# SwiGLU feed-forward: gate 0 moves to SyncE's queue, and ScalarE loads its table before its one load

## The chip, the core and the metric

The kernel runs on one core of a Trainium2 chip. A core has TensorE (matrix multiply, with a separate row for its weight loads), VectorE, ScalarE, GpSimd and SyncE. ScalarE and SyncE can both issue DMAs, each on a queue of its own; SyncE does nothing else here. The metric is the device time of one execution in microseconds, given as the median over several runs.

## The reference

The inputs are x (2048 tokens of 512 values), w_gate and w_up (512 x 1376) and w_down (1376 x 512), all in bf16:

```python
g = silu(x @ w_gate)
u = x @ w_up
return (g * u) @ w_down
```

## The kernel before

The kernel works with transposed activations: for each tile of 128 features it computes x @ w transposed, features on the partitions and tokens along the free dimension. Weights are the stationary operand and the transposed x, `xT_sb`, is the moving one. The 512 values of the contraction make four steps (`dk`) of 128, so one tile of 128 features by 512 tokens takes four matmuls into one PSUM bank. The features make ten full tiles and a rest of 96; gate and up of one tile use two banks of the eight. ScalarE applies silu to the gate bank, VectorE multiplies with the up bank and writes `hT_sb`. There are four chunks of 512 tokens; after them the rest of 96 features is handled in groups X and Y. The second stage multiplies with w_down in pieces of 32 partitions and stores 16 output tiles of 128 tokens.

What concerns the change is the start. Tokens 256 and up come transposed by a DMA (`load_x`, line 95). Tokens 0-127 and 128-255 come in their natural layout (`load_xn`, line 115, into `xn_sb`) and are transposed by TensorE with an identity matrix (line 367); VectorE and ScalarE copy the four tiles of each block to `xT_sb` in turn. The weights of the first stage come in slabs, `[(0, 1), (1, 2), (2, 4), (4, 7), (7, 11)]` in tiles of 128 features, each with one gate and one up load (line 100). Gate 0 and up 0 below are the first slab: 128 KB each.

The order is written out by hand. Before the change ScalarE's queue issues gate 0 and tokens 128-255, then a small dummy activation (line 277), whose only purpose is that ScalarE loads its function table (the ACT_TABLE_LOAD in the profile) before silu is needed. Then its list of operations starts, each waiting for TensorE. SyncE's queue issues tokens 0-127, up 0, then slabs 1 and 2-3, the transposing loads of tokens 256-383 and 384-511, the other slabs, the other tokens, w_down, and last the output stores.

TensorE begins with seven matmuls on constants (`warm`, line 358) that compute nothing that is used. Then, each step waiting only for what it reads:

- transposes of tokens 0-127, and two more constant matmuls
- gate 0 on tokens 0-127 (needs gate 0, line 326)
- transposes of tokens 128-255
- up 0 on tokens 0-127 (needs up 0)
- gate 0 and up 0 on tokens 128-255
- six tiles of slabs 1 and 2-3 on tokens 0-255, in the order gate 1, up 1, gate 2, gate 3, up 2, up 3
- gate 0 and up 0 on tokens 256-383, then on 384-511, then the other six tiles on tokens 256-511
- all other tiles on 512 tokens at once.

A load is awaited once, by the first matmul that needs it (`need`). A bank is used again when its readers are done (`free`). GpSimd makes the indices from which VectorE builds the identity, and has no load on its queue.

Of the kernel before, what the change touches and what calls it, by code (L numbers as in the profile page):

```python
# [14 lines left out]
def bass_standalone__swiglu_ffn__prompt_kernel(nc, x, w_gate, w_up, w_down, out):  # L15
# [35 lines left out]
    with ExitStack() as es:  # L51
# [33 lines left out]
        def load_sem(name):  # L85
            loads[name] = sem(f"s_{name}")
            return loads[name]
# [6 lines left out]
        def load_x(eng, name, t0, t1):  # L94
            eng.dma_start_transpose(
                xT_sb[:, :, t0:t1], xf[t0:t1, :]
            ).then_inc(load_sem(name), 16)

        def load_w(eng, name, src, base, f0, f1):
            eng.dma_start(  # L100
                w_sb[:, :, base + f0:base + f1],
                src[:, f0:f1].rearrange("(k p) f -> p k f", p=P),
            ).then_inc(load_sem(name), 16)

        slabs = [(0, 1), (1, 2), (2, 4), (4, 7), (7, NFT)]
        slab_of = {ft: a for a, b in slabs for ft in range(a, b)}

        def load_gate(eng, a, b):
            load_w(eng, f"wg{a}", w_gate, 0, a * P, min(b * P, F))

        def load_up(eng, a, b):
            load_w(eng, f"wu{a}", w_up, UPH, a * P, min(b * P, F - 32))

        def load_xn(eng, i):
            eng.dma_start(xn_sb[:, i, :], xf[i * P:(i + 1) * P, :]).then_inc(load_sem(f"xn{i}"), 16)
# [1 line left out]
        def out_rows(t):  # L117
            return of[t * P:(t + 1) * P, :]

        def loads_on_scalar(act):  # L120
            load_gate(act, *slabs[0])
            load_xn(act, 1)

        def loads_on_sync(sp):
            load_xn(sp, 0)
            load_up(sp, *slabs[0])
            for a, b in slabs[1:3]:
                load_gate(sp, a, b)
                load_up(sp, a, b)
            load_x(sp, "x0b", HT, HT + P)  # L130
            load_x(sp, "x0c", HT + P, SC)
            for a, b in slabs[3:]:
                load_gate(sp, a, b)
                load_up(sp, a, b)
            load_w(sp, "wut", w_up, F - (F - 32), F - 32, F)
            for c in range(1, NSC):
                load_x(sp, f"x{c}", c * SC, (c + 1) * SC)
            sp.dma_start(
                wd_sb[:, 0:NFF, :], w_down[0:NFF * P, :].rearrange("(k p) d -> p k d", p=P)
            ).then_inc(load_sem("wd"), 16)  # L140
            load_sem("wdt")
            for y0 in (0, 64):
                sp.dma_start(wd_sb[y0:y0 + 64, T01, :], w_down[NFF * P:F - SR, :]).then_inc(loads["wdt"], 16)
            for x0 in range(0, P, SR):
                sp.dma_start(wd_sb[x0:x0 + SR, T2, :], w_down[F - SR:F, :]).then_inc(loads["wdt"], 16)
            sp.dma_start(wd_sb[0:F_LAST, TAIL, :], w_down[NFF * P:F, :]).then_inc(load_sem("wdl"), 16)
# [104 lines left out]
        def ready(op):  # L251
            return op["ready"] if "ready" in op else (s_P, op["g"]["at"] + 1)

        def store_tiles(eng, own):
            for o, t, c0, c1, ob, copied, n in stores:
                if o == own:
                    eng.wait_ge(s_A if copied == "A" else s_D, n)
                    eng.dma_start(out_rows(t)[:, c0:c1], o_sb[ob][:, c0:c1]).then_inc(s_out[ob], 16)

        def on_sync(sp):  # L260
            loads_on_sync(sp)
            store_tiles(sp, "S")
            for i in range(NOS):
                sp.wait_ge(s_out[i], 16 * n_store[i])
# [8 lines left out]
            pool.tensor_copy(hl_sb[64:96, :], hx_sb[64:96, c, SC - P:SC]).then_inc(s_L, 1)  # L273

        def on_scalar(act):
            loads_on_scalar(act)
            act.activation(adummy[:, 0:4], zero_c, ACT.Silu)  # L277
            for op in act_ops:
                act.wait_ge(*ready(op))
                if op["kind"] == "silu":  # L280
                    if op["free"]:
                        act.wait_ge(s_D, op["free"])
                    fn = ACT.Silu
                else:
                    if op["stored"][1]:
                        act.wait_ge(*op["stored"])
                    fn = ACT.Copy
                act.activation(op["out"], op["src"], fn).then_inc(s_A, 1)  # L288
            store_tiles(act, "A")
# [199 lines left out]
        on_sync(nc.sync)  # L489
        on_gpsimd(nc.gpsimd)  # L490
        on_scalar(nc.scalar)
        on_tensor(nc.tensor)
        on_vector(nc.vector)
# [28 lines left out]
```

## Time and profile before

| what | value |
|---|---|
| time, median of 3 runs | 120.14 us (120.06 to 120.38) |
| the profiled execution's own time | 120.41 us |
| its span, first to last instruction | 119.1 us |
| TensorE busy | 116.5 us (98%) |
| VectorE busy | 38.3 us (32%) |
| ScalarE busy | 35.2 us (30%) |
| TensorE's first matmul starts | 0.77 us |
| table load on ScalarE | starts 1.79 us, takes 1.28 us |
| DMA read and written | 4.75 MB and 2.10 MB |

The profile is of one execution. Engines are PE (TensorE's matmuls), PEld (its weight loads), DVE (VectorE), ACT (ScalarE), POOL (GpSimd) and SP (SyncE). A name with q behind it (ACTq, SPq) is the engine's instruction queue, which issues DMAs and handles waits. The length of a DMA line is the time that the queue took to issue it; the data land later, and the page gives the time from the start of the issue to the landing. L326 is line 326 of the kernel. Matmuls overlap each other, so the length of one is longer than its distance to the next; the distance, or the number of matmuls in a window, tells the rate. A remark in square brackets is the time that the engine sat idle just before, and what ended it.

### The profile page before, as it was taken

How to read it: one execution, taken by the hardware profiler on the slowest of the kernel's cores; microseconds unless marked ns; L12 is line 12 of the kernel's file. 1: busy time of each engine (PE TensorE's matmuls, PEld its weight loads, DVE VectorE, ACT ScalarE, POOL GpSimd, SP SyncE). 2: the span in 40 equal slices, each digit the busy share in tenths (PEclk: the TensorE clock that was granted, in tenths of full speed). 3: DMA queues.
4: the chain of work that ended last, by engine and by line, in shares of the span. 5: the costliest groups of instructions: out<-in, count | busy, mean ns of one | idle time of the engine just before them, and what ended most of it. 6: DMA issues, size and time to landing. Idle time of an engine off the chain costs nothing.

```text
span 119.1 us, 2344 instructions
## 1 busy us (share of the span) xinstructions
PE 116.5 (98%) x1019; PEld 60.6 (51%) x1019; DVE 38.3 (32%) x61; ACT 35.2 (30%) x62; POOL 1.0 (1%) x7
## 2 busy tenths in 40 slices
PE   7999999999999999999999999999999999999993
PEld 2899544444444444444444444444444445885452
DVE  0204633444334444334453344361000044003321
ACT  3406444262343272442353432430000033003021
POOL 1000000000000000000000000001000000000000
DMA  4999989991000000000000000000000017200612
GB/s 84 296 176 347 265 178 239 265 340 29 0 6 0 0 0 0 0 6 0 0 0 6 0 0 0 0 0 6 0 6 0 0 51 235 77 0 6 204 61 88
DMA packets 17642, 8.83 MB, mean 74 GB/s; under 512 B 10624, under 2 KB 17632, under 8 KB 17632
## 3 DMA queue, kind: packets, MB, share of 16 engines
q1 hardware_dynamic: 16816, 8.33, 27.5%
q10 hardware_dynamic: 816, 0.36, 1.1%
q8 instruction: 8, 0.13, 0.4%
q14 instruction: 2, 0.02, 0.1%
HBM read 4.75 MB, written 2.10 MB: 58 GB/s over the span
## 4 chain that ended last, share of the span: by engine, by line
PE 98%; DVE 0%; issue 0%
PE bank L326 62%; PE bank L444 25%; PE bank L483 7%; PE bank L358 2%; PE bank L406 2%; PE bank L367 1%; DVE o_sb L302 0%
## 5 line engine op out<-in xcount | busy, mean ns | idle before, releaser
L326 PE MATMUL bank<-xT_sb,w_sb 128*128 128x512 bf16 (+2 forms) x384 | 73.7, 356 | 0.0
L326 PEld LDWEIGHTS bank<-xT_sb,w_sb 128*128 128x128 bf16 x384 | 37.0, 100 | 36.3
L298 DVE TENSOR_TENSOR hT_sb<-sg_sb,bank 128x512 bf16<-128x512 f32 x40 | 27.5, 687 | 40.5 <-PE bank L326 39.6
L288 ACT ACTIVATE sg_sb<-bank 128x512 f32<-128x512 f32 x40 | 23.8, 596 | 40.9 <-PE bank L326 40.8
L444 PE MATMUL bank<-wd_sb,hT_sb 32*128 32x512 bf16 x496 | 29.0, 374 | 0.0
L444 PEld LDWEIGHTS bank<-wd_sb,hT_sb 32*128 32x128 bf16 x496 | 15.2, 93 | 11.6 <-issue 0.4
L302 DVE CAST o_sb<-bank 128x512 bf16<-128x512 f32 (+1 forms) x10 | 5.7, 595 | 31.1 <-PE bank L444 25.9
L288 ACT ACTIVATE o_sb<-bank 128x512 bf16<-128x512 f32 (+1 forms) x8 | 4.3, 582 | 33.6 <-PE bank L444 27.9
L483 PE MATMUL bank<-wd_sb,hT_sb 128*128 128x512 bf16 (+2 forms) x56 | 8.1, 304 | 0.0
L483 PEld LDWEIGHTS bank<-wd_sb,hT_sb 128*128 128x128 bf16 x56 | 4.2, 97 | 4.2 <-issue 0.4
L444 PE MATMUL bank<-wd_sb,hy_sb 32*128 32x512 bf16 (+1 forms) x32 | 5.0, 371 | 0.0
L298 DVE TENSOR_TENSOR hx_sb<-sgx_sb,bank 32x512 bf16<-32x512 f32 x4 | 2.8, 692 | 3.5 <-ACT sgx_sb L288 3.5
L288 ACT ACTIVATE sgx_sb<-bank 32x512 f32<-32x512 f32 x4 | 2.3, 587 | 4.5 <-PE bank L326 4.5
L358 PE MATMUL bank<-const-bfloat16-1.0 128*128 128x512 bf16 (+1 forms) x9 | 2.9, 486 | 0.8 <-PEq L507 0.8
L444 PE MATMUL bank<-wd_sb,hx_sb 32*128 32x512 bf16 (+1 forms) x16 | 3.0, 371 | 0.0
L288 ACT ACTIVATE sgy_sb<-bank 64x512 f32<-64x512 f32 x4 | 2.4, 590 | 0.1
L358 PEld LDWEIGHTS bank<-const-bfloat16-1.0 128*128 128x128 bf16 x9 | 1.1, 140 | 2.1 <-issue 2.1
L406 PE MATMUL bank<-xT_sb,w_sb 128*64 128x512 bf16 x16 | 1.9, 382 | 0.0
L444 PEld LDWEIGHTS bank<-wd_sb,hy_sb 32*128 32x128 bf16 x32 | 1.6, 93 | 0.6
L302 DVE COPY xT_sb<-bank 128x128 bf16<-128x128 bf16 x4 | 0.9, 224 | 3.0 <-PE bank L367 3.0
L277 ACT ACT_TABLE_LOAD x1 | 1.3, 1283 | 1.8 <-issue 1.8
L406 PEld LDWEIGHTS bank<-xT_sb,w_sb 128*64 128x64 bf16 x16 | 0.8, 109 | 1.0 <-DVE hT_sb L298 0.4
(16 smaller groups left out, 7.3 us busy)
## 6 DMA issues: line engine op xcount, KB each, us to landing
out_dram<-o_sb SPq DMA_DIRECT2D x15, 128.0 KB, 1.8
wd_sb<-in_w_down_dram SPq DMA_DIRECT2D x1, 1280.0 KB, 8.3
w_sb<-in_w_gate_dram SPq DMA_DIRECT2D x1, 480.0 KB, 5.5
w_sb<-in_w_up_dram SPq DMA_DIRECT2D x1, 448.0 KB, 7.5
w_sb<-in_w_gate_dram SPq DMA_DIRECT2D x1, 384.0 KB, 4.0
w_sb<-in_w_up_dram SPq DMA_DIRECT2D x1, 384.0 KB, 4.4
w_sb<-in_w_up_dram SPq DMA_DIRECT2D x2, 128.0 KB, 3.3
w_sb<-in_w_gate_dram SPq DMA_DIRECT2D x1, 256.0 KB, 3.7
```

The costliest lines, as they stand in the source:

```text
L277: act.activation(adummy[:, 0:4], zero_c, ACT.Silu)
L288: act.activation(op["out"], op["src"], fn).then_inc(s_A, 1)
L298: ins = dve.tensor_tensor(op["out"], op["a"], op["b"], ALU.mult)
L302: ins = dve.tensor_copy(op["out"], op["src"])
L326: return pe.matmul(bank[:, n0:n1], lhsT=w_sb[:, dk, col:col + P], rhs=xT_sb[:, dk, c * SC + n0:c * SC + n1], start=(dk == 0), stop=(dk == ...
L358: pe.matmul(banks[NB - 1][:, 0:width], lhsT=ones_w, rhs=ones_m[:, 0:width], start=True, stop=True)
L367: pe.matmul(tview(i, dk), lhsT=xn_sb[:, i, dk * P:(dk + 1) * P], rhs=ident[:, :], start=True, stop=True, is_transpose=True,).then_inc(s_X, 1)
L406: ins = pe.matmul(g["bank"][y0:y1, :], lhsT=w_sb[:, dk, YC0:YC0 + 64], rhs=xT_sb[:, dk, c * SC:(c + 1) * SC], start=(dk == 0), stop=(dk == ...
L444: ins = pe.matmul(g["bank"][:, 0:c1 - c0], lhsT=h, rhs=wd_sb[r0:r0 + SR, w, c0:c1], start=(start and fk == fks[0]), stop=(stop and fk == f ...
L483: ins = pe.matmul(g["bank"][:, 0:c1 - c0], lhsT=h, rhs=w, start=(last and fk == 0), stop=(fk == (NFF if last else NFF - 1)), skip_group_ch ...
```

## The change

ScalarE no longer issues gate 0. It starts with the dummy activation, and with it the table load, and then issues the load of tokens 128-255. SyncE issues tokens 0-127, gate 0, up 0 and then everything that it issued before in the same order. No computation and no wait of another engine is changed.

```diff
-        def loads_on_scalar(act):
-            load_gate(act, *slabs[0])
-            load_xn(act, 1)
-
         def loads_on_sync(sp):
             load_xn(sp, 0)
-            load_up(sp, *slabs[0])
-            for a, b in slabs[1:3]:
+            for a, b in slabs[0:3]:
                 load_gate(sp, a, b)
                 load_up(sp, a, b)
             load_x(sp, "x0b", HT, HT + P)
...
         def on_scalar(act):
-            loads_on_scalar(act)
             act.activation(adummy[:, 0:4], zero_c, ACT.Silu)
+            load_xn(act, 1)
             for op in act_ops:
                 act.wait_ge(*ready(op))
```

## The prediction

> **What bounds the kernel now.** I read the chain of waits first, then the first ten microseconds of the timeline with the DMA issues, and last TensorE's groups in two short windows. All times are from the profiled execution, which took 120.41 us: its span of 119.1 us and 1.3 us around it. That is 0.27 us above the median of the runs shown, 120.14 us, so I sum differences and set them on the median. About 0.3% (0.36 us) is what a measurement of this kernel can tell from no change.
>
> The busy line and the chain of waits, in order of time (start, length, what):
>
> ```profile
> PE 116.5 (98%) x1019; PEld 60.6 (51%) x1019; DVE 38.3 (32%) x61; ACT 35.2 (30%) x62; POOL 1.0 (1%) x7
> ...
> 0.77 2.51 PE bank L358 x7
> 3.28 0.01 issue
> 3.29 0.58 PE bank L367 x4
> 3.88 0.21 PE bank L358 x2
> 4.09 0.46 PE bank L326 x4
> 4.55 0.47 PE bank L367 x4
> 5.01 72.96 PE bank L326 x380
> ```
>
> The chain is TensorE from end to end. From 5 us on it never leaves TensorE, so a load matters only if it makes TensorE wait, and everything that the change moves is needed in the first ten microseconds. Here is what is issued and done there (start, length, engine, line):
>
> ```profile
> 0.74 0.46 ACTq L100 DMA_DIRECT2D w_sb<-in_w_gate_dram  x1
> 0.74 0.40 SPq L115 DMA_DIRECT2D xn_sb<-in_x_dram  x1
> 1.19 0.42 SPq L100 DMA_DIRECT2D w_sb<-in_w_up_dram  x1
> 1.23 0.53 ACTq L115 DMA_DIRECT2D xn_sb<-in_x_dram  x1
> 1.79 1.28 ACT L277 ACT_TABLE_LOAD   x1 [1.79 <-issue]
> 3.08 0.20 ACT L277 ACTIVATE act_dummy<-const-float32-0.0 128x4 f32<-128x4 f32 x1
> 3.26 0.35 PEld L367 LDWEIGHTS bank<-ident,xn_sb 128*128 128x128 bf16 x4 [0.25 <-issue]
> 3.70 0.49 ACT L288 ACTIVATE xT_sb<-bank 128x128 bf16<-128x128 bf16 x2 [0.41 <-PE bank L367]
> 3.93 0.41 PEld L326 LDWEIGHTS bank<-xT_sb,w_sb 128*128 128x128 bf16 x4
> 4.40 0.34 PEld L367 LDWEIGHTS bank<-ident,xn_sb 128*128 128x128 bf16 x4
> 4.70 0.15 PEld L326 LDWEIGHTS bank<-xT_sb,w_sb 128*128 128x128 bf16 x1
> ```
>
> And the issues of 0.5 to 2.9 us with their size and the time from issue to landing:
>
> ```profile
> w_sb<-in_w_gate_dram ACTq DMA_DIRECT2D x1, 128.0 KB, 2.9
> xn_sb<-in_x_dram SPq DMA_DIRECT2D x1, 128.0 KB, 2.4
> xn_sb<-in_x_dram ACTq DMA_DIRECT2D x1, 128.0 KB, 3.1
> ```
>
> Together they give the landings. Tokens 0-127 land at 0.74 + 2.4 = 3.14 and their transposes (line 367) load weights at 3.26, so TensorE waited for them. Gate 0 lands at 0.74 + 2.9 = 3.64, 0.29 us ahead of its first weight load at 3.93, which waits for a transposed tile instead. Tokens 128-255 land at 1.23 + 3.1 = 4.33, and their transposes load weights at 4.40: just in time. Up 0 lands at 1.19 + 3.3 = 4.49 (3.3 is the median of both up loads of 128 KB) and is needed at 4.70.
>
> TensorE's rate in this stretch is read from two windows, 4.8 to 5.9 us and 6.1 to 8.6 us:
>
> ```profile
> L326 PE MATMUL bank<-xT_sb,w_sb 128*128 128x128 bf16 x11 | 1.4, 312 | 0.0
> L326 PE MATMUL bank<-xT_sb,w_sb 128*128 128x256 bf16 x24 | 2.8, 273 | 0.0
> ```
>
> Eleven matmuls of 128 columns took 1.1 us, and 24 of 256 columns 2.6 us (0.109 each): from about 6.0 us on TensorE does twice the columns in the same time. Before that it is at half rate.
>
> **The change, part by part.**
>
> 1. Tokens 0-127 stay SP's first issue at 0.74. Their companion on the other queue becomes tokens 128-255 (128 KB in rows of 1 KB) instead of gate 0 (128 KB in rows of 256 bytes). Earlier by at most TensorE's idle 0.25 us before 3.26; later by at most the 0.44 us that 128 KB take at the 296 GB/s of the window 2.6 to 6.0 us. The same bytes compete as before, so I take 0.
>
> 2. Gate 0 moves from ScalarE's first issue at 0.74 to SP's second at 1.19. With its own 2.9 us it lands at 4.09; with the 3.3 us of up 0, which had this place, queue and shape, at 4.49. The reaction at 4.40 followed a landing by 0.07, so its weight load moves from 3.93 to 4.16 or 4.56: +0.2 to +0.6. Up 0 is the nearest row, but it shared its time with gate 0, which now isn't beside it; I take the middle, +0.4.
>
> 3. Tokens 128-255 are ScalarE's only load, behind the table load and the dummy activation. The trace has no DMA issue behind a table load. If the queue merely hands both to the engine, the issue starts at about 0.80 and lands at 3.2 to 3.9 (2.4 or 3.1 us), before gate 0: cost 0. If it stands behind both (1.28 + 0.20 us), it starts at 0.74 + 1.48 = 2.22 and lands at 4.6 to 5.3, and the transposes of 4.40 go to 4.7 to 5.4: +0.3 to +1.0, not added to part 2 but taking its place where larger. Two rows speak for handing over. The dummy activation starts at 3.08, 0.01 us after the table load's end (1.79 + 1.28 = 3.07), so it was already waiting in the engine. And near the end ScalarE's queue handles a semaphore at 109.3 (line 286) that stands between two output copies, the first running from 109.24 and the second starting at 109.7. I take 0 and keep +1.0 for the range.
>
> 4. The table load itself comes forward by about 1 us and gains nothing: it and the dummy end at 3.28, and ScalarE's first real work at 3.70 waits 0.41 us for the transposes. That slack covers it and grows; without it the first tile copies would be late by what the 1.48 us overran.
>
> 5. Up 0 moves to 1.66 and lands at 1.66 + 3.3 = 4.96. Its weight load, at 4.70 plus 0.4 from part 2, is at 5.10. Covered; with the smaller delay of part 2 it would set +0.33 itself.
>
> 6. All later SP issues slip by one issue, 1.66 - 1.19 = 0.47 us (up to 0.55 further on), and each is checked against TensorE's first use after the shift of 0.2 found below. Gate 2-3 (2.75, 3.7 us): 6.45 becomes 7.00 against 6.06 + 8 x 0.109 + 0.2 = 7.13. Up 2-3 (3.30, 3.9): 7.20 becomes 7.75 against 8.00. Tokens 256-383 (3.85, 4.1): 7.95 becomes 8.50 against 8.88. Tokens 384-511 (5.24, 3.1): 8.34 becomes 8.89 against 9.33. The next gate slab (6.54, 4.0): 10.54 becomes 11.1 against 12.4. The tightest margin is 0.13 us, so 0; with no shift at all gate 2-3 would stall TensorE by 0.13 or so. The queue's longest wait is for output copies after the loads, so the slip goes no further.
>
> The sum to the first use of up 0 is +0.4 us of waiting. What it costs at the end depends on the rate. If the step to full rate stays at about 6.0 us, the work pushed past it runs in half the time, and half of the wait comes back: +0.2. If the step moves with the work, +0.4. I take +0.2, since the change leaves TensorE's start at 0.77 and its seven fill matmuls alone. In the profiled execution that would be 120.6, on the median 120.14 + 0.2 = 120.35 us: inside what can't be told from no change, near its upper edge.
>
> [...]
>
> **The rivals.**
>
> *ScalarE's queue stands behind the table load* (slower). Place: the issue of line 115. For it: no row shows a queue passing a table load. Against it: the two rows of part 3. Price: TensorE's second transposes at 4.7 to 5.4. At the late end up 0's first matmul goes from 4.81 to 5.81; of the 12 half-rate matmuls up to 6.06 two run before 6.0 and ten at 0.056 (0.109 for 256 columns, halved), ending near 6.6: +0.5. Over both ends and with the rate's step moving along, +0.15 to +1.0, most likely 120.5 to 120.7. It decides from an issue later than about 1.6 us.
>
> *The full rate comes later* (slower). Place: the half-rate stretch before 6.0. Part 2 adds 0.2 to 0.6 us of idling to the 0.25 us that TensorE now idles there. If the step wants TensorE kept busy for as long as it was here (0.77 to 6.0, 5.2 us) counted from the end of the wait at 4.3, it comes at 9.5, and 3.5 us of full-rate work take twice as long, half of it lost: up to +1.75 and the 0.4, 122.3; a step only 1 us later costs 0.5, 120.85. For it: idling grows where the rate is decided. Against it: the step came although TensorE paused at 3.2, 3.9 and 4.4. It decides if the new idle is more than the step tolerates, which no row shows. [...]
>
> *The first tokens come sooner* (faster). The window 0.7 to 2.6 us moved 73 GB/s, so tokens 0-127 may land earlier with other company. Price: at most the 0.25 us of idle, if gate 0 lands by 3.7, only 2.5 us after its issue; halved, 120.0. To be faster by over 0.36 us the rate's step must come earlier too.
>
> **How the numbers follow.** The forecast has 0.45: 0.36 within 0.3%, 0.09 above it (part 2 at its upper end with no halving). The held-up queue has 0.25: 0.06 within, 0.19 slower. The late rate has 0.19, all slower. The sooner tokens have 0.11: 0.08 faster, 0.03 within. Sums: faster 0.08, within 0.45, slower 0.47. The forecast's own range is 120.1 to 120.6. The range from 119.9 to 121.5 takes in the held-up queue and the smaller half of the late rate, and leaves out some 0.16: its larger half, a few of the held-up queue, and most of the faster cases.
>
> **What would show it.** Right: line 115 on ScalarE's queue at 0.8, beside a table load at 0.74; gate 0's first weight load at 4.2 to 4.5; the second transposes 0.45 us behind it with no wait for the tokens; matmuls of 256 columns at 0.109 from about 6.25. The queue rival shows as line 115 after 2.0, the late rate as 256 columns at 0.21 beyond 6.3. A wait inside line 326 between 7 and 9.5 would say that part 6 was wrong. A delay of up 0's first matmul other than 0.4, or a step of the rate that moves, makes the prediction wrong.

## The result, and the profile after

| | before | after |
|---|---|---|
| median of 14 runs each | 120.22 us | 120.88 us |
| lowest and highest | 119.96 and 120.82 | 120.41 and 122.96 |
| ratio after to before, 95% interval | | 1.004 [1.002, 1.0059] |
| the profiled execution's own time | 120.41 us | 120.58 us |
| its span | 119.1 us | 119.2 us |

The changed kernel is slower by about 0.4%, or 0.48 us (0.004 x 120.2). Three of its 14 runs took 122.3 us or more, over 1.5% above its fastest, and the ratio leaves them out: with them the medians are 0.66 us and the means 0.88 us apart.

The profiled execution after lies 0.30 us below the median of its kernel, the one before 0.19 us above that of its own. So the two profiles show less than the difference, and it has to be read from their first ten microseconds. Rows from the timeline after (start, length, engine, line; line 115 is still the load of tokens in natural layout, 271 is the dummy activation, 362 the transposes, 321 the first stage's matmuls; other rows are left out):

```profile
0.74 0.39 SPq L115 DMA_DIRECT2D xn_sb<-in_x_dram  x1
0.74 1.28 ACT L271 ACT_TABLE_LOAD   x1 [0.74 <-PEq L502]
0.81 0.38 ACTq L115 DMA_DIRECT2D xn_sb<-in_x_dram  x1
1.19 0.42 SPq L100 DMA_DIRECT2D w_sb<-in_w_gate_dram  x1
1.66 0.50 SPq L100 DMA_DIRECT2D w_sb<-in_w_up_dram  x1
2.04 0.20 ACT L271 ACTIVATE act_dummy<-const-float32-0.0 128x4 f32<-128x4 f32 x1
3.41 0.34 PEld L362 LDWEIGHTS bank<-ident,xn_sb 128*128 128x128 bf16 x4 [0.40 <-issue]
3.85 0.96 SPq L100 DMA_DIRECT2D w_sb<-in_w_up_dram  x1
4.08 0.41 PEld L321 LDWEIGHTS bank<-xT_sb,w_sb 128*128 128x128 bf16 x4
4.40 0.31 PEld L362 LDWEIGHTS bank<-ident,xn_sb 128*128 128x128 bf16 x4
5.39 1.44 PEld L321 LDWEIGHTS bank<-xT_sb,w_sb 128*128 128x128 bf16 x20 [0.67 <-DMA w_sb<-in_w_up_dram]
7.02 0.77 PEld L321 LDWEIGHTS bank<-xT_sb,w_sb 128*128 128x128 bf16 x8 [0.19 <-DMA w_sb<-in_w_gate_dram]
7.95 1.10 PEld L321 LDWEIGHTS bank<-xT_sb,w_sb 128*128 128x128 bf16 x12 [0.17 <-DMA w_sb<-in_w_up_dram]
```

ScalarE's load goes out at 0.81, beside the running table load. TensorE starts the first transposes and gate 0 0.15 us late and is back on time at the second transposes, 4.40. Then its weight loads sit idle three times: 0.67 us for up 0, 0.19 us for gate 2-3, 0.17 us for up 2-3. The DMA issues of 1.6 to 1.7 us with the time to landing (the view also lists gate 0, whose issue ends at 1.61):

```profile
w_sb<-in_w_gate_dram SPq DMA_DIRECT2D x1, 128.0 KB, 2.8
w_sb<-in_w_up_dram SPq DMA_DIRECT2D x1, 128.0 KB, 3.7
```

Gate 0 landed at 1.19 + 2.8 = 4.0, up 0 only at 1.66 + 3.7 = 5.4. The chain of waits now starts on SyncE's queue and goes through up 0 (two of its rows):

```profile
1.66 3.69 DMA w_sb<-in_w_up_dram
5.39 72.74 PE bank L321 x380
```

The DMA traffic shows what up 0 met. Three stretches (from and to, length, granted clock, mean busy share of the DMA engines where transfers overlap, GB/s), first of the kernel before, then after:

```profile
3.00:3.40 0.40, 1.00 1.25 312
3.40:4.20 0.80, 1.00 1.19 305
4.20:5.00 0.80, 1.00 1.26 273
```

```profile
3.00:3.40 0.40, 1.00 1.20 280
3.40:4.20 0.80, 1.00 0.52 78
4.20:5.00 0.80, 1.00 1.11 240
```

From 3.4 to 4.2 us the changed kernel moves a quarter of what the kernel before moves. Both token loads are through (3.31 and 3.62), gate 0 ends (3.97), ScalarE's queue has nothing more (no packet of it moves in this stretch), and SyncE's third load, up 0, has hardly begun: from 3.4 us to gate 0's landing SyncE's queue moves 168 packets, with the end of gate 0 among them, and up 0 alone has 512 (128 KB in rows of 256 bytes).

TensorE's rate after, from the matmuls of line 321 between 5.3 and 5.9 us:

```profile
L321 PE MATMUL bank<-xT_sb,w_sb 128*128 128x128 bf16 x9 | 0.7, 220 | 0.5 <-DMA w_sb<-in_w_up_dram 0.5
```

These nine matmuls of 128 columns take the time from 5.39 to 5.90 us, under 0.06 each: full rate, where before it was 0.1 up to 6.0 us. By the distances of the matmuls the step came at about 4.5 us. That is why the six tiles on 256 tokens begin at 6.07 us here and at 6.06 in the profile before, in spite of the waits.

### The profile page after: what moved, and what is told of

Same layout as the page of the kernel before. It is cut to its first block, busy times and chain, and to the rows that moved or that the text cites. A ratio compares the mean times of both kernels' runs of the same rounds, so it can differ in the third digit from the quotient of the medians.

```text
span 119.2 us, 2344 instructions
## 1 busy us (share of the span) xinstructions
PE 116.0 (97%) x1019; PEld 59.7 (50%) x1019; DVE 38.2 (32%) x61; ACT 35.1 (29%) x62; POOL 1.0 (1%) x7
## 4 chain that ended last, share of the span: by engine, by line
PE 94%; DMA 3%; SPq 1%; issue 0%; DVE 0%
PE bank L321 61%; PE bank L439 25%; PE bank L478 7%; DMA w_sb<-in_w_up_dram 3%; PE bank L401 2%; SPq L100 0%; SPq L115 0%; DVE o_sb L297 0%
## 5 line engine op out<-in xcount | busy, mean ns | idle before, releaser
L321 PEld LDWEIGHTS bank<-xT_sb,w_sb 128*128 128x128 bf16 x384 | 36.1, 98 | 37.3 <-DMA w_sb<-in_w_up_dram 0.8
L283 ACT ACTIVATE xT_sb<-bank 128x128 bf16<-128x128 bf16 x4 | 0.9, 276 | 2.1 <-PE bank L362 2.1
```

Of the source, the lines that this page charges most:

```text
L321: return pe.matmul(bank[:, n0:n1], lhsT=w_sb[:, dk, col:col + P], rhs=xT_sb[:, dk, c * SC + n0:c * SC + n1], start=(dk == 0), stop=(dk == ...
```

## The experiments

Each ratio is to the kernel before, run beside it on the same chip. Landings are those of one profiled execution. Where a diff adds a load into `extra_sb`, the tile itself and a wait for the load at the end of the kernel are left out of the diff.

### Table load first, and nothing else

```diff
-            loads_on_scalar(act)
             act.activation(adummy[:, 0:4], zero_c, ACT.Silu)
+            loads_on_scalar(act)
```

> Only the order on ScalarE's queue changes: dummy activation with the table load first, then gate 0 and tokens 128-255; SyncE as before. Theory A (late arrivals: up 0 lands 0.8 us later and all SyncE loads slip, the table load itself is free): gate 0 is issued at about 0.81 instead of 0.74 and tokens 128-255 at about 1.3, so the time is that of before within 0.1 us. Rival B (putting the table load ahead of the loads costs something itself): slower than before by 0.3 to 0.5 us. Rival C (the late or early step to full rate decides): no more idle on TensorE than before, so as before.

Measured: 1.001 [0.999, 1.0031]. The order on ScalarE costs nothing that can be told, which speaks against rival B.

### Table load last, gate 0 still on SyncE

```diff
-            act.activation(adummy[:, 0:4], zero_c, ACT.Silu)
             load_xn(act, 1)
+            act.activation(adummy[:, 0:4], zero_c, ACT.Silu)
```

(The diff is to the changed kernel.)

> The changed kernel with the table load put back behind ScalarE's load of tokens 128-255; SyncE still issues gate 0. Theory A: as the changed kernel, 0.4 to 0.6 us above before, up 0's first matmul at about 5.4. Rival B: back to before, within 0.2 us. Rival C: as the changed kernel.

Measured: 1.0058 [1.0031, 1.0084], as the changed kernel within the intervals. With the run before it, rival B is out: the place of the table load does not make the loss, so the new order of the loads does. The profiled execution took 122.58 us, and its matmuls of 256 columns between 7.05 and 9.2 us, and those between 9.72 and 10.8 us, were:

```profile
L321 PE MATMUL bank<-xT_sb,w_sb 128*128 128x256 bf16 x11 | 2.5, 420 | 0.0
```

```profile
L321 PE MATMUL bank<-xT_sb,w_sb 128*128 128x256 bf16 x12 | 1.5, 273 | 0.0
```

The eleven start 0.21 us apart, half rate; the twelve 0.11 apart, full rate. The step came at about 9.5 us. This is what the late-rate rival of the prediction looks like.

### Up 0 third

```diff
-            load_up(sp, *slabs[0])
-            for a, b in slabs[1:3]:
-                load_gate(sp, a, b)
-                load_up(sp, a, b)
+            load_gate(sp, *slabs[1])
+            load_up(sp, *slabs[0])
+            load_up(sp, *slabs[1])
+            load_gate(sp, *slabs[2])
+            load_up(sp, *slabs[2])
```

> The kernel before with two of SyncE's issues exchanged: gate 1 goes second and up 0 third, everything from up 1 on stays in its place, gate 0 stays on ScalarE. This delays up 0 alone. Theory A in the form that the wait for up 0 is the cost: up 0 lands at 5.0 to 5.35, TensorE waits 0.3 to 0.6 us for it, and the time rises by 0.15 (half comes back through the rate's step) to 0.6 us. Theory A in the form that the slip of all later loads is the cost: within 0.1 us of before.

Measured: 1.0006 [0.9983, 1.0028], although up 0 landed at 5.14 and TensorE waited for it:

```profile
5.19 3.81 PEld L327 LDWEIGHTS bank<-xT_sb,w_sb 128*128 128x128 bf16 x36 [0.31 <-DMA w_sb<-in_w_up_dram]
```

So a late up 0 alone makes no loss that can be told from none, though the interval reaches up to 0.34 us. The long run of weight loads behind it has no further wait.

### A slip of the later loads

```diff
             load_up(sp, *slabs[0])
+            sp.dma_start(extra_sb[:, :], xf[0:P, 0:64]).then_inc(load_sem("extra"), 16)
             for a, b in slabs[1:3]:
```

> The kernel before with one small extra load (128 rows of 128 bytes into a tile that nothing reads) on SyncE's queue right behind up 0, so that all later SyncE loads are issued about 0.4 us later while up 0, gate 0 and the tokens 0-255 keep their places. Slip form of theory A: TensorE waits between 6.5 and 9.5 us for slabs 2-3 or tokens 384-511, and the time rises by 0.2 to 0.5 us. Up 0 form: within 0.1 us of before, as the margins of 0.1 to 0.4 us of the prediction hold.

Measured: 1.002 [1.0001, 1.004], 0.24 us, at the lower end of what the slip form expected. TensorE now waits for gate 2-3:

```profile
6.74 2.88 PEld L329 LDWEIGHTS bank<-xT_sb,w_sb 128*128 128x128 bf16 x35 [0.25 <-DMA w_sb<-in_w_gate_dram]
```

In this execution the full rate came at about 5.3 us, so TensorE was there sooner than in the profile before. The margins that the prediction read from one execution depend on that.

### Up 0 on ScalarE's queue

```diff
-            for a, b in slabs[0:3]:
+            load_gate(sp, *slabs[0])
+            for a, b in slabs[1:3]:
                 load_gate(sp, a, b)
                 load_up(sp, a, b)
...
             load_xn(act, 1)
+            load_up(act, *slabs[0])
```

(To the changed kernel.)

> The changed kernel with up 0 moved to ScalarE's queue behind tokens 128-255; SyncE issues tokens 0-127, gate 0, and then slab 1 on in the places that they had before the change. Theory A (the wait for up 0 and the slip of SyncE's later loads add up to the loss): up 0 is issued at about 1.2 instead of 1.66 and lands by 4.9 instead of 5.35, the later loads land as before, and the time is within 0.2 us of before. Rival D (the loss comes from tokens 0-127 and 128-255 being loaded side by side, which makes both and what follows later): stays 0.3 to 0.6 us above before.

Measured: 1.0027 [1.0003, 1.0051]. Up 0 landed at 4.81, as expected; the time is 0.32 us above before, outside the 0.2 of theory A and at the lower edge of rival D. Waits are left for gate 0 (0.42 us) and gate 2-3 (0.33). The interval is wide, and the time settles little. The landings say more against rival D: with the two token loads side by side, tokens 0-127 landed at 3.05, earlier than before (3.15).

### ScalarE's two loads exchanged

```diff
-            load_gate(act, *slabs[0])
             load_xn(act, 1)
+            load_gate(act, *slabs[0])
```

(To the kernel before.)

> The kernel before with ScalarE's two loads exchanged: tokens 128-255 first, beside tokens 0-127 on SyncE, then gate 0; SyncE as before. Rival D: tokens 0-127 land 0.15 to 0.6 us later than in the kernel before (first transposes at 3.4 to 3.9 instead of 3.3), and the time rises by 0.2 to 0.4 us. Theory A: gate 0 lands at about 4.1 and costs 0.1 us, up 0 and the later loads keep their places: within 0.15 us of before.

Measured: 1.0046 [1.0024, 1.0067], as much as the change itself, with SyncE's issues untouched. Tokens 0-127 landed at 3.51, their transposes loaded weights at 3.61 instead of 3.26, gate 0 landed at 4.50 and kept TensorE idle for another 0.37 us. Here the tokens came late as rival D said, and its 0.2 to 0.4 us overlaps the interval (0.29 to 0.81 us). But in the changed kernel, with the same two loads side by side, the first transposes were 0.15 us late in one profile and 0.03 in the other, so this is not its main term.

This kernel and the one before it issue loads of the same sizes on the same queues in the same order, with gate 0 and up 0 exchanged, and with ScalarE's first issue at 0.74, ahead of the table load, instead of 0.81, behind it. Yet gate 2-3 landed at 7.21 here and at 6.68 there. Whether the 0.07 us, the exchanged weights or mere scatter makes that difference was not tested, so a single landing should be read with some tenths of a microsecond of doubt.

### TensorE's wait filled

```diff
             transposes(1)
+            for i in range(6):
+                pe.matmul(banks[2][:, 0:P], lhsT=ones_w, rhs=ones_m[:, 0:P], start=True, stop=True)
             gu_matmuls(first[1], 0, P)
```

(To the changed kernel.)

> The changed kernel with six more matmuls of 128 columns on constants in TensorE's wait for up 0 (0.64 us at half rate, 0.34 at full rate). If the loss comes from the idle stretch holding back the step to full rate, it shrinks by at least 0.3 us and the times of single runs lie closer together. If it comes from late data alone (theory A), the median is as in the changed kernel within 0.15 us.

Measured: 1.0076 [1.0057, 1.0095], no gain. By its median of 120.97 us it is the changed kernel, as the second form expected; by the ratio it loses 0.91 us against 0.48, with intervals that just overlap. Idling that holds back the rate is not what makes the loss in the compared runs. From up 1 on the loads landed later still in its profile, and the waits moved on:

```profile
7.04 0.33 PEld L321 LDWEIGHTS bank<-xT_sb,w_sb 128*128 128x128 bf16 x4 [0.45 <-DMA w_sb<-in_w_up_dram]
7.84 1.21 PEld L321 LDWEIGHTS bank<-xT_sb,w_sb 128*128 128x128 bf16 x12 [0.46 <-DMA w_sb<-in_w_gate_dram]
```

Its six runs lay between 120.77 and 121.34 us, closer together than those of the changed kernel. The first form expected that too, but six runs are few.

### Loads spread over both queues

```diff
+            act.activation(adummy[:, 0:4], zero_c, ACT.Silu)
             loads_on_scalar(act)
-            act.activation(adummy[:, 0:4], zero_c, ACT.Silu)
+            load_up(act, *slabs[1])
```

(To the kernel before; SyncE no longer issues up 1.)

> ScalarE does the table load first and then issues gate 0, tokens 128-255 and up 1; SyncE issues tokens 0-127, up 0, gate 1 and then slab 2-3 and all else one place earlier than before. Theory A: the loads that TensorE waits for between 6.5 and 9.5 us when the full rate comes early land up to 0.5 us sooner, and the time falls by 0.1 to 0.3 us. If the 16 DMA engines were already full and not the issue order the limit: within 0.1 us of before.

Measured: 1.0021 [0.9997, 1.0045]. It is no faster, against theory A; the interval holds the 0.1 us of the other expectation. Gate 2-3 landed at 6.98, not sooner than before (6.43), though it was issued 0.55 us earlier.

### A slip in front of up 0

```diff
+            sp.dma_start(extra_sb[:, :], xf[0:P, 0:64]).then_inc(load_sem("extra"), 16)
             load_up(sp, *slabs[0])
             for a, b in slabs[1:3]:
```

> The kernel before with the small extra load of 128 rows of 128 bytes in front of up 0 on SyncE's queue: up 0 becomes SyncE's third issue and everything behind it slips, as in the changed kernel, but ScalarE keeps gate 0 and tokens 128-255, so its queue has data to move while SyncE's third load starts. Theory E (the DMA engines run half empty from 3.4 to 4.2 us in the changed kernel, because ScalarE's queue has nothing left): the window 3.4 to 4.2 us moves over 200 GB/s, up 0 lands by 5.1, and the time rises by 0.2 to 0.3 us, as with the slip alone. Theory A (places in SyncE's queue alone): up 0 lands at 5.3 or later and the time rises by 0.4 to 0.7 us, as in the changed kernel.

Measured: 1.0029 [1.0012, 1.0047]. Up 0 landed at 4.87 and the time rose by 0.35 us, near theory E; the window of 3.4 to 4.2 us moved 154 GB/s, below the 200 that it expected.

### Up 1 on ScalarE's queue

```diff
-            for a, b in slabs[0:3]:
-                load_gate(sp, a, b)
-                load_up(sp, a, b)
+            load_gate(sp, *slabs[0])
+            load_up(sp, *slabs[0])
+            load_gate(sp, *slabs[1])
+            load_gate(sp, *slabs[2])
+            load_up(sp, *slabs[2])
...
             load_xn(act, 1)
+            load_up(act, *slabs[1])
```

(To the changed kernel.)

> The changed kernel with up 1 moved from SyncE to ScalarE behind tokens 128-255. Up 0 stays SyncE's third issue; gate 1 keeps the slipped place, and slab 2-3 and all later loads are back in their places of before. Theory E: up 1 fills part of the empty stretch of 3.4 to 4.2 us (over 150 GB/s instead of 78), so that the later loads land within 0.2 us of before although up 0 is still late, and half or more of the loss goes: 0 to 0.3 us above before. Theory A in the up 0 form: up 0 still lands at 5.2 or later and the time stays 0.4 to 0.7 us above before.

Measured: 1.004 [1.0016, 1.0063], median 121.22 us. The empty stretch was filled, and it did not help. The window of 3.4 to 4.2 us and TensorE's wait:

```profile
3.40:4.20 0.80, 1.00 1.26 279
```

```profile
6.18 2.86 PEld L324 LDWEIGHTS bank<-xT_sb,w_sb 128*128 128x128 bf16 x33 [1.51 <-DMA w_sb<-in_w_up_dram]
```

Up 0 took 4.5 us from its issue and landed at 6.14, while up 1, not needed for long, was there at 4.54. Gate 2-3 landed at 7.34. The 0.48 us and the late up 0 are what theory A's up 0 form expected, though up 0 third had spoken against that form. Theory E falls as it was put: a busy stretch alone does not bring the later loads in.

### The changed kernel again

No edit.

> The changed kernel itself beside the other two, for the comparison on one chip and for a second look at when TensorE's full rate comes. All theories: 0.4 to 0.7 us above before, 77 to 120 GB/s in the window 3.4 to 4.2 us, up 0 landing at 5.3 to 5.8. If the step to full rate is tied to the work, it comes again just after gate 0's first matmuls (4.45 us); if it is not, it comes at another time.

Measured: 1.0045 [1.0023, 1.0067], 76 GB/s in the stretch, up 0 after 3.9 us at 5.57:

```profile
5.61 1.44 PEld L321 LDWEIGHTS bank<-xT_sb,w_sb 128*128 128x128 bf16 x20 [1.06 <-DMA w_sb<-in_w_up_dram]
7.24 0.77 PEld L321 LDWEIGHTS bank<-xT_sb,w_sb 128*128 128x128 bf16 x8 [0.20 <-DMA w_sb<-in_w_gate_dram]
```

The step to full rate came between 3.8 and 4.1 us, at the latest between gate 0's second and third matmul (0.06 us apart, where the first profile has 0.10), and not at its fourth as in the first profile. So it is not tied to the work.

### Only the tokens late

```diff
+            for i in range(2):
+                sp.dma_start(extra_sb[:, i, :], xf[i * P:(i + 1) * P, 0:64]).then_inc(load_sem(f"extra{i}"), 16)
             load_x(sp, "x0b", HT, HT + P)
```

> The kernel before with two small extra loads (128 rows of 128 bytes each) on SyncE's queue between up 2-3 and the transposing load of tokens 256-383. Gate 0, up 0, slabs 1 and 2-3 keep their places and only the tokens from 256 on and what follows come later, tokens 384-511 at 8.9 to 9.2 us instead of 8.34. Theory F (over the runs so far the time goes with the landing of tokens 384-511, the last load of the first chunk, and not with that of up 0): the time rises by 0.3 to 0.5 us although up 0 is as early as before. Rival (the wait for up 0 and for slab 2-3 is what costs): within 0.1 us of before.

Measured: 1.0023 [1.0009, 1.0038], 0.28 us, just under theory F and above its rival. It does not separate them as it was meant to, because in its profile gate 2-3 came late too (6.82), and that is what TensorE waited for:

```profile
6.87 2.75 PEld L331 LDWEIGHTS bank<-xT_sb,w_sb 128*128 128x128 bf16 x34 [0.35 <-DMA w_sb<-in_w_gate_dram]
```

### What they show together

The times at which the loads had landed in each kernel's profile, by the trace's landing events; the time at which the distances of the matmuls show the full rate; TensorE's wait for gate 2-3; and the measured ratio:

| kernel | up 0, us | gate 2-3, us | full rate, us | wait for gate 2-3, us | ratio |
|---|---|---|---|---|---|
| before | 4.53 | 6.43 | 6.0 | none | 1 |
| table load first | 4.41 | 6.38 | 6.0 | none | 1.001 |
| up 0 third | 5.14 | 6.58 | 6.6 | none | 1.0006 |
| up 0 on ScalarE | 4.81 | 6.68 | 4.8 | 0.33 | 1.0027 |
| slip | 4.49 | 6.70 | 5.3 | 0.25 | 1.002 |
| only the tokens late | 4.41 | 6.82 | 5.4 | 0.35 | 1.0023 |
| after | 5.35 | 6.98 | 4.5 | 0.19 | 1.004 |
| spread | 4.16 | 6.98 | 6.0 | none | 1.0021 |
| slip in front of up 0 | 4.87 | 7.02 | 6.5 | none | 1.0029 |
| after, again | 5.57 | 7.20 | 3.8 to 4.1 | 0.20 | 1.0045 |
| exchanged | 4.17 | 7.21 | 7.0 | none | 1.0046 |
| up 1 on ScalarE | 6.14 | 7.34 | 3.7 | none | 1.004 |
| table load last | 5.76 | 7.44 | 9.5 | none | 1.0058 |
| filled | 5.54 | 7.80 | 5.4 | 0.46 | 1.0076 |

Over these 14 rows the ratio goes with the landing of gate 2-3 (correlation 0.95) and much less with that of up 0 (0.57). A straight line through them gives 0.59 us of time per microsecond of gate 2-3. For the change, 6.43 to 6.98 or 7.20 makes 0.32 to 0.45 us of the 0.48. This was found after the runs and rests on one profile per row, and tokens 384-511 land late in the same kernels (8.34 before, 8.97 after; correlation 0.93).

The columns of the full rate and of the wait show what joins the landing to the time. All six profiles with a wait for gate 2-3 reached the full rate by 5.4 us, and none of the seven that reached it at 6.0 us or later waited, even where gate 2-3 landed at 7.44. In the profile that is left, up 1 on ScalarE with the full rate at 3.7 us, TensorE had already waited 1.51 us for up 0. So a late gate 2-3 makes TensorE wait in executions with an early step. That these are about half of the executions would fit the slope of 0.59, but only one execution of each kernel was profiled.

The loss arises early: from the first matmul of the first stage on 512 tokens to the end of the span it is 106.7 or 106.9 us in all 14 profiles. That the whole train of SyncE's loads from up 0 on comes late in the changed kernel is shown; which load of the train decides is open, and so is why the third load of SyncE starts so slowly. None of the kernels beat the one before.

## Why the prediction was right or wrong

The range of 119.9 to 121.5 holds 120.88, and slower had the larger chance by a little. That is partly luck. The single time, 120.35, is 0.5 us low, the forecast's own range of 120.1 to 120.6 does not hold the result, and the upper part of the range was there for a held-up queue, which did not happen, and for the late rate, which the 0.48 us does not contain. By its own signs the prediction was wrong: up 0's first matmul came 0.58 us later than before (5.39 instead of 4.81; 0.80 in the second profile) and not 0.4, the rate's step moved, and TensorE waited at 7.02 and 7.95.

1. *First tokens, taken as 0.* Their transposes loaded weights at 3.41 instead of 3.26, 0.15 us later, and 0.03 later in the second profile. Near enough.

2. *Gate 0, +0.4.* Over-sized. It landed 2.8 us after its issue, faster than by either row that bounded it, and its weight load went from 3.93 to 4.08, all of which is the lateness of the tokens.

3. *Tokens 128-255, 0 if ScalarE's queue hands over.* Right: issued at 0.81 and landed at 0.81 + 2.8 = 3.6. The two rows were read rightly, and the held-up queue is out. The dummy again started within 0.02 us of the table load's end (2.04 against 0.74 + 1.28 = 2.02), and the issue came 0.07 us after the table load's start.

4. *Table load, 0.* Right, by the first two experiments.

5. *Up 0, covered.* This step failed. It gave up 0 a flight of 3.3 us from loads that had the other queue's traffic around them; it took 3.7 and 3.9 us, landed at 5.35 and 5.57 instead of 4.96, and TensorE sat idle for 0.67 and 1.06 us.

6. *The slip, covered by 0.13 us and more.* This step failed too, and seems to carry more of the loss: the slip alone cost 0.24 us and a late up 0 alone 0.07, though the intervals overlap. The margins were measured from one execution whose full rate came at 6.0 us. Gate 2-3 landed where the step said (6.98 against 7.00) and TensorE still waited 0.19 us for it, 0.17 us more for up 2-3. So the term is not 0. The step also missed that SyncE's issue of up 2-3 took 0.96 us instead of 0.51, so that the first transposing load went out at 4.85 instead of 3.85; it landed at 8.50 all the same, where the step had put it.

7. *The rate's step at about 6.0 us, so that half of the wait comes back.* Wrong premise. The step is neither at a fixed time nor tied to the work. In the profiles of these kernels it lies between 3.7 and 9.5 us: 6.0, 5.3 and 5.4 us in the kernel before, in the slip and in the one with late tokens, whose first four microseconds are the same work; about 4.5 and 4 us in the two profiles of the changed kernel. With an early step no half-rate work is left in which the waits could come back, and in the changed kernel's profile the loads set the pace until 7.95 us. What sets the time of the step, no run here shows.

8. *The late-rate rival, 0.19.* It was seen in one profile: a step at 9.5 us and 122.58 us, close to the 9.5 and 122.3 of the prediction. Its working does not hold, though. It wanted TensorE busy for 5.2 us from the end of the wait, and there the wait ended at 5.81, which would make 11.0; with up 1 on ScalarE's queue the step came 2.9 us after TensorE's first matmul, so 5.2 us are not needed. Runs above 122 us occur in just those six rows of the table whose TensorE sat idle for 0.3 us or more (0.31 to 1.51) for up 0 in the profile: in 13 of their 67 runs, and in none of the 76 of the other seven changed rows or of the kernel before. That fits the rival, but only one such run was profiled and it was not tested by itself. The 0.48 us is not from it, being worked out from runs of 121.2 us and less; over all runs, where the means are 0.88 us apart, it would be some 0.4.

## What to carry to other kernels

When a load moves between queues, count not only its own arrival but that of every load behind it (here gate 2-3 landed at 6.98 and 7.20 instead of 6.43), and take its flight time from a load in the same place with the same neighbours, not from a median (here 3.7 and 3.9 us instead of 3.3). A margin of a few tenths read from one execution is no cover where the rate's step moves from run to run (here from 3.7 to 9.5 us). A wait at the start need not show in the time (up 0 third waited 0.31 us at a ratio of 1.0006), so delay each load alone before naming the cause.

## What was not expected of the hardware

Near the start of the kernel a load further back on SyncE's queue began later after its issue. The first was issued at 0.74 and its first packet moved at 1.77 us, 1.03 us later, before and after the change. The second, issued at 1.19, moved its first at 2.76 before and 2.88 after, 1.57 and 1.69 us later. In the kernel with the slip, the third, issued at 1.67 and told apart by its rows of 128 bytes, moved its first packet at 3.62, 1.95 us later.

In the changed kernel, with one load on ScalarE's queue, the DMA engines were half busy from 3.4 to 4.2 us (0.52 and 78 GB/s, where before it was 1.19 and 305). Filling that stretch from ScalarE's queue (279 GB/s) came with an up 0 that landed at 6.14 instead of 5.35. The slip in front of up 0 fell to 154 GB/s with two loads on ScalarE's queue, so their number is not the whole reason. The change put up 0's issue 0.47 us later (1.66 instead of 1.19), and up 0 landed 0.82 to 1.04 us later (5.35 and 5.57 instead of 4.53).

TensorE kept its full rate through a long wait: with up 1 on ScalarE's queue the full rate came at 3.7 us, TensorE then sat idle for 1.51 us, and its matmuls from 6.25 to 6.81 are 0.06 apart, still the full rate.

The column of the granted clock reads 1.00 throughout, also where the distance of equal matmuls is twice as long; TensorE's rate had to be read from the matmuls. The same kernel's runs spread over about 1 us (119.89 to 120.88 for the kernel before in one comparison).
